# Finishing an item's maxima on VectorE and GpSimd, with at most three maxima in an attention group and one burst more in an MLP's first step

## The chip, the core and the metric

The kernel runs on one core of a Trainium2 chip. The core has a matrix engine (TensorE, here PE, with its weight loads as PEld), a vector engine (VectorE, DVE), an engine for activation functions (ScalarE, ACT), a general one (GpSimd, POOL) and one that here only issues DMAs (SyncE, SP). Each works through its own instructions in order; semaphores tie them together. Matrix products land in PSUM, eight banks of 128 × 512 float32; everything else on the chip lies in SBUF. The metric is device time in microseconds (us), the median over several runs.

## The reference

One transformer layer on 2048 rows of width 512, in float32: softmax attention with 32 heads of width 16, and then an MLP of width 1792 with SiLU, each behind a LayerNorm and added to its input.

```
x = A_x                                        # (1, 2048, 512)
h  = x + A_ref(layernorm(x), wqkv, wo)         # 32 heads of 16, no mask
h2 = h + B_ref(layernorm(h), w1, w2)           # silu(h @ w1) @ w2
A_ref: q, k, v = split(x @ wqkv); p = softmax(q @ k.T * 16**-0.5); (p @ v) @ wo
```

## The kernel before

**Stages.** First LayerNorm, transposition and the projections to q, k and v, for all rows. Queries and keys are split into a high and a low half-precision part and parked in DRAM (`qd`, `kd`). Then attention, in 32 *items*: an item is one block of 512 query rows and four heads, so eight items make a block of rows. After each block come the output projection, the second LayerNorm and the MLP for its 512 rows; those of blocks 0 to 2 lie inside attention, that of the last block at the end. The MLP of a block runs after the first 16 groups of the next block's first item, that is, at groups 144, 272 and 400 (`marks`, L670); the output projection lies in the groups just before.

**An attention group.** An item is 16 groups, one for each 128 keys, 512 groups in all, numbered g. In a group (L714 to L723) PE forms for each of the four heads the scores of 128 keys against 512 queries (`scores`, bank `ps_s`), ACT takes the exponential into `pt` (L81), and two groups later four heads' value products are added into the bank `pv` (`values`, L67). Products with `pt` are in float32, and each is recorded as two instructions, so a group has eight of them.

**The maxima.** The exponential needs the row maximum of each query's scores beforehand, so the same scores are formed once more, in the other orientation and ahead of time: `maximum` (L198) forms 128 queries against 512 keys on PE in one of three banks `ps_m` and DVE reduces it to one number (L206). An item has 64 of these. Two heads use the lower and the upper half of the matrix engine's rows; inside a group a maximum is issued right behind the scores of a head on the other half, and the two run at the same time. When an item's 64th maximum is out, `finish_max` (L210) reduces four numbers to one for each row and head (`nm`, L213), scales it and splits it into a high and a low half-precision part (`ns`, L216 and L217). Two *ticks* later (`WAIT = 2`; a tick is a group, or a step of an MLP) `place_max` (L222) transposes `ns` on PE (L70), copies it with ACT (`mt`, L227) and writes it with four DMAs on SP's queue (L231) into the rows of the item's queries `qs`, from where the score product itself subtracts the maximum. The scores of an item wait for these four DMAs. Queries and keys of five items are on the chip at a time (`RING`).

**Who forms how many maxima, and when.** 212 of the 2048 are formed in the projections. In an MLP, `weave` counts products and calls `burst(3)` at each eighth (`BESIDE_C = 8, 3`). An MLP's step f (14 of them) has twelve products of the first layer and, from f = 1, twelve of the second for f − 1. In attention a planner, `maxima(g)` (L672), says how many maxima a group gets:

```
rate = max([(64 * (n + 1) - BESIDE * sum(g <= m <= KC * n for m in marks) - at["done"])
            / max(1, KC * n - AHEAD - g) for n in range(i + 1, ITEMS)] or [0])
```

So each later item n has to be through with its maxima `AHEAD` groups before its first group, 16 n, with `BESIDE` maxima counted as done in each MLP that lies between. The largest of these demands is the rate; what it amounts to is saved up in `due`, and whole maxima are taken from it, at most four in a group. The order of the program is fixed: every instruction is issued in the order of the text on its engine.

**GpSimd's part.** It multiplies the attention output by the inverse sums (`divide`, L513) once in two items, after waiting for the DMA of `den`; in the MLPs of blocks 0 to 2 it forms the low parts of the weights, `w1l` and `w2l`, with a subtraction of two 128 × 512 tiles each (L74). In the small statistics of the LayerNorm it forms `rs` in two steps.

Of the kernel before, what the change touches and what calls it, by code (L numbers as in the profile page):

```python
# [14 lines left out]
ALU = mybir.AluOpType  # L15
# [21 lines left out]
MX = 2.0 ** 15  # L37
# [8 lines left out]
ITEMS = NB * H // 4  # L46

WAIT = 2
AHEAD = 6


BESIDE = 123
OUTPUT = 9

BESIDE_A = 7, 4
# [4 lines left out]
def attention_mlp_kernel(ctx: ExitStack, tc: tile.TileContext, x, wqkv, wo, w1, w2, out):  # L60
    nc = tc.nc
# [11 lines left out]
    def pool(op, *a, **k):  # L73
        tc.keep_in_program_order(getattr(nc.gpsimd, op)(*a, **k))  # L74


    def pin(ins):
        tc.keep_in_program_order(ins)

    def act(fn, *a, **k):  # L80
        pin(getattr(nc.scalar, fn)(*a, **k))  # L81

    def dve(fn, *a, **k):
        pin(getattr(nc.vector, fn)(*a, **k))  # L84

    def dma(*a):
        pin(nc.sync.dma_start(*a))  # L87

    def low(dst, src, high, engine="dve"):

        if engine == "pool":
            pool("tensor_tensor", dst, src, high.bitcast(F32), ALU.subtract)
        else:
            dve("tensor_tensor", dst, src, high.bitcast(F32), ALU.subtract)
# [6 lines left out]
    def product(ps, lh, ll, rh, rl, n, start=True, stop=True):  # L101

        k = 0
        for c in range(n):
            for a, b in ((lh, rh), (ll, rh), (lh, rl)):
                mm(ps, a(c), b(c), start=start and k == 0, stop=stop and k == 3 * n - 1)
                k += 1
                yield
# [11 lines left out]
    def bank(name, kind="st", dtype=F32):  # L120
        return banks[kind].tile([P, 512], dtype, tag=kind, name=name)
# [88 lines left out]
    def finish_max(i):  # L210

        nm = small.tile([P, 16], F32, name="nm")
        pin(nc.vector.tensor_reduce(nm, mx.pop(i).rearrange("p j a q k -> p (j a q) k"), axis=AX.X, op=ALU.max,  # L213
                                    negate=True))
        ns = small.tile([P, 2, 16], F16, name="ns")
        pin(nc.vector.tensor_scalar(ns[:, 0, :], nm, 1.0 / MX, None, op0=ALU.mult))  # L216
        pin(nc.vector.scalar_tensor_tensor(ns[:, 1, :], nm, 1.0 / MX, ns[:, 0, :], op0=ALU.mult, op1=ALU.subtract))  # L217
        return ns

    placed = set()  # L220
# [18 lines left out]
    at = {"item": 0, "done": 0, "half": 0, "products": 0, "step": 0, "due": 0, "mlp": False}  # L239
# [6 lines left out]
    def tick():  # L246
        at["step"] += 1
        for fn, a in agenda.pop(at["step"], ()):
            fn(*a)
# [6 lines left out]
    def one_max(half=None):  # L256

        i = next_item()
        if i == ITEMS:
            return  # L260
        if half is None:
            half = at["half"]
            at["half"] = 1 - half
        half = half if todo[i, half] else 1 - half
        at["done"] += 1
        if maximum(*todo[i, half].pop(0)):
            soon(WAIT, place_max, i, finish_max(i))
# [5 lines left out]
    def weave(steps, beside):  # L273

        for _ in steps:
            at["products"] += 1
            if beside and at["products"] % beside[0] == 0:
                burst(beside[1])


    with ExitStack() as pa:
# [142 lines left out]
        for g in range(1, NG // 2):  # L424
            for m, (b, key) in enumerate([(b, 1) for b in range(NB)] + [(b, 0) for b in range(NB)]):
# [4 lines left out]
                n = 8 * g + m - 12  # L430
# [92 lines left out]
    def load_weights(kind, f):  # L523
        if f < FC:
            w = raw_w[kind, f] = gp.tile([P, 512], F32, tag="w", name="w", bufs=4)
            if kind == "w1":
                dma(w.rearrange("p (c n) -> p c n", n=P), w1[:, f * P:(f + 1) * P].rearrange("(c p) n -> p c n", p=P))
            else:
                dma(w, w2[f * P:(f + 1) * P, :])

    def split_weights(kind, f, engine):
        if f < FC:
            w = raw_w.pop((kind, f))
            wh, wl = ws[kind, f] = [gp.tile([P, 512], F32R, name=kind + part) for part in "hl"]
            act("copy", wh, w)
            low(wl, w, wh, engine)
# [20 lines left out]
    def rows_of(b, t):  # L557
        return ot[b % 2][:, t].rearrange("p c n -> p (c n)")
# [10 lines left out]
    def mlp(b, beside):  # L569
        engine = "pool" if beside else "dve"  # L570

        first = bank("ps_w1")
        acc = [bank("ps_acc") for _ in range(3)]

        def second(f, gh, gl):
            w2h, w2l = ws.pop(("w2", f))
            if f == 0:
                acc.append(bank("ps_acc"))
            for t in range(4):
                weave(product(acc[t], lambda c: gh[:, t * P:(t + 1) * P], lambda c: gl[:, t * P:(t + 1) * P],  # L580
                              lambda c: w2h, lambda c: w2l, 1, start=f == 0, stop=f == FC - 1),
                      beside if f < FC - 1 else None)
                if f == FC - 1:
                    n = 4 * b + t
                    h = rows_of(b, t)
                    dve("tensor_tensor", h, acc[t], h, ALU.add)
                    dma(out[n * P:(n + 1) * P, :], h)

        last = None
        at["products"] = 0  # L590
        for f in range(FC):
            tick()
            load_weights("w1", f + 2)
            load_weights("w2", f + 1)
            w1h, w1l = (w.rearrange("p (c n) -> p c n", n=P) for w in ws.pop(("w1", f)))
            split_weights("w1", f + 1, engine)
            split_weights("w2", f, engine)
            ps = pv if f else first
            weave(product(ps, lambda c: w1h[:, c, :], lambda c: w1l[:, c, :],
                          lambda c: hth[:, c, :], lambda c: htl[:, c, :], DC), beside)  # L600
            g, gh, gl = (bp.tile([P, 512], dt, tag="pt", name=name)
                         for name, dt in (("g", F32), ("gh", F32R), ("gl", F32R)))
            act("activation", g, ps, AF.Silu)
            act("copy", gh, g)
            low(gl, g, gh)
            if last:
                second(*last)
            last = (f, gh, gl)
        if b < NB - 1:

            act("activation", small.tile([P, 1], F32, name="sw"), ident[:, :1], AF.Exp)
        second(*last)
# [14 lines left out]
    def finish_block(b, pending):  # L627

        act("activation", small.tile([P, 1], F32, name="sw"), ident[:, :1], AF.Silu)
        for g in pending:  # L630
            values(g)
        at["mlp"] = True
        mlp(b, BESIDE_C)
        at["mlp"] = False

    def finish_last(pending):
# [29 lines left out]
        for t in range(4):  # L666
            turn_rows(t)
        mlp(b, None)

    marks = [KC * (8 * b + 1) for b in range(1, NB)]  # L670

    def maxima(g):  # L672

        i, c = divmod(g, KC)
        if g < LAG:
            return 0
        ready = min(ITEMS, i + RING - (0 if c == KC - 1 else 1)) * 64
        rate = max([(64 * (n + 1) - BESIDE * sum(g <= m <= KC * n for m in marks) - at["done"])
                    / max(1, KC * n - AHEAD - g) for n in range(i + 1, ITEMS)] or [0])
        if ready < END:  # L680
            rate = min(rate, (ready - at["done"]) / (KC - 1 - c or KC))
        at["due"] += max(0, rate)
        n = max(0, min(4, int(at["due"]), ready - at["done"]))
        at["due"] -= n
        return n

    fixed_rows(RING - 1)
    for g in range(groups):
# [10 lines left out]
        if i in (8, 16, 24):  # L699
            b, n = i // 8 - 1, c - OUTPUT  # L700
# [8 lines left out]
        if g == groups - 4:  # L709
            for t in range(4):  # L710
                load_rows(NB - 1, t)
            for w in first_weights.values():
                load_weights(*w)
        n = maxima(g)  # L714
        for m in range(4):
            k = m ^ (g % 2)
# [41 lines left out]
```

## Time and profile before

| | |
|---|---|
| runs (three) | 1754.59, 1755.76 (median), 1760.3 us |
| the profiled execution | 1754.43 us, of which the span is 1752.7 |
| mean granted TensorE clock in it | 0.992 |
| projections of q, k, v and the start | to about 208 us |
| attention with three MLPs inside | about 208 to 1643 us |
| output and MLP of the last block | from about 1643 us |
| DVE, small operations of 32 items: L213, L216, L217 | 220, 209, 203 ns mean |
| of these, the longest single ones | 222, 886, 1061 ns |

The profile is one execution recorded instruction by instruction. A line of a time list gives the start, the time from the start of the first to the end of the last of a run of like instructions, engine, line of the kernel, operation, output and input with their shapes, and how many; in brackets stands how long the engine had been idle before and for whom. A table by stretches gives start and end, the length, then for each engine that has such instructions the busy time and their number, and last the granted clock, the DMA engines' share and GB/s. Instructions overlap on an engine: a matmul of 0.4 us is followed by the next after 0.23.

### The profile page before, as it was taken

Reading aid. Unit: us, or ns where it says so; the run is one execution under the profiler, and the core shown is the slowest. Engines: PE = TensorE matmul, PEld = TensorE weight load, DVE = VectorE, ACT = ScalarE, POOL = GpSimd, SP = SyncE. Lnnn points to the kernel's source line nnn. Section 1 sums busy time; section 2 is a strip of 40 time slices with the busy share of each in tenths; the row PEclk is TensorE's granted clock in tenths of the full one; section 3 lists DMA queues with packets and bytes.
Section 4 is the critical chain, followed back from the end, with each engine's and each line's share of the span. In section 5 each row is a group of like instructions: output and inputs, shape, how many; then the busy total and the mean of one; then the engine's idle time right before and its main releaser. Section 6 shows DMA issues by size and latency. Waiting matters only on the chain.

```text
span 1752.7 us, 28228 instructions
## 1 busy us (share of the span) xinstructions
PE 1699.7 (97%) x10466; PEld 654.2 (37%) x10466; DVE 1472.0 (84%) x2456; ACT 1263.3 (72%) x2507; POOL 208.4 (12%) x216
## 2 busy tenths in 40 slices
PE   7899999999999999999999999999999999999899
PEld 6655422222245532222245532222245532221377
DVE  6889899999978889999978899999978889994243
ACT  4223499999963369999963269999963279999643
POOL 2112210000033300000033300000033200000000
PEclk9999999999999999999999999999999999999999
DMA  6233311111113111111213111111222111100232
GB/s 183 91 87 137 113 36 44 38 39 48 51 52 100 57 45 32 35 41 44 58 48 100 55 48 30 35 45 40 61 69 82 49 45 34 36 8 11 64 90 74
DMA packets 102210, 103.10 MB, mean 59 GB/s; under 512 B 20344, under 2 KB 78776, under 8 KB 102072
## 3 DMA queue, kind: packets, MB, share of 16 engines
q1 hardware_dynamic: 102072, 101.30, 19.8%
q8 instruction: 82, 1.34, 0.3%
q14 instruction: 56, 0.46, 0.1%
HBM read 77.86 MB, written 17.30 MB: 54 GB/s over the span
## 4 chain that ended last, share of the span: by engine, by line
PE 46%; ACT 33%; DVE 18%; DMA 1%; issue 1%; SPq 1%; POOL 0%; ACTq 0%; POOLq 0%; DVEq 0%
ACT pt L81 31%; PE pv L67 20%; DVE mx L206 13%; PE ps_s L67 9%; PE ps_m L67 6%; PE ps_acc L67 5%; PE ps_wo L67 2%; DVE gl L84 2%; PE ps_v L67 2%; PE ps_qk L67 1%; ACT pvs L81 1%; DVE ot L84 1%; SPq L87 1%; PE ps_tr L70 1%; DMA w<-in_B_w_dram 0%
## 5 line engine op out<-in xcount | busy, mean ns | idle before, releaser
L206 DVE TENSOR_REDUCE mx<-ps_m 128x1 f32<-128x512 f32 x2048 | 1280.4, 683 | 114.2 <-PE ps_m L67 87.8
L81 ACT ACTIVATE pt<-ps_s 128x512 f32<-128x512 f32 x2048 | 1017.7, 646 | 31.9 <-PE ps_m L67 31.4
L67 PE MATMUL ps_s<-qs,ks 64*128 64x512 f16 x2048 | 549.9, 380 | 10.6 <-ACT pt L81 2.4
L67 PE MATMUL ps_m<-ks,qs 48*128 48x512 f16 x2048 | 531.1, 381 | 11.6 <-DVE mx L206 8.9
L67 PE MATMUL pv<-pt,va 128*17 128x512 f32 x4096 | 539.0, 599 | 0.9
L67 PEld LDWEIGHTS <-ks 64*128 64x128 f16 x2048 | 152.4, 94 | 549.9 <-issue 443.5
L67 PEld LDWEIGHTS pv<-pt,va 128*17 128x17 f32 x4096 | 68.8, 95 | 240.3 <-issue 225.9
L67 PEld LDWEIGHTS <-qs 48*128 48x128 f16 x2048 | 122.1, 94 | 82.8 <-issue 77.1
L81 ACT ACTIVATE g<-pv 128x512 f32<-128x512 f32 x52 | 31.1, 597 | 146.3 <-PE pv L67 146.3
L74 POOL TENSOR_TENSOR ot<-ot,den 128x512 f32<-128x512 f32 x15 | 19.1, 1275 | 938.3 <-DMA den<-dr 938.3
L84 DVE TENSOR_TENSOR gl<-g,gh 128x512 fp32r<-128x512 f32 x56 | 59.0, 1053 | 44.1 <-ACT gh L81 44.1
L67 PE MATMUL ps_acc<-w2h,gh 128*128 128x512 f32 x224 | 92.3, 412 | 0.0
L67 PE MATMUL ps_acc<-w2l,gh 128*128 128x512 f32 x224 | 91.6, 409 | 0.0
L81 ACT CAST w2h<-w 128x512 fp32r<-128x512 f32 x56 | 34.8, 621 | 75.2 <-POOL w1l L74 38.7
L67 PE MATMUL ps_acc<-w2h,gl 128*128 128x512 f32 x224 | 88.1, 393 | 0.0
L67 PE MATMUL pv<-hth,w1l 128*128 128x512 f32 x208 | 86.6, 416 | 0.0
L67 PE MATMUL pv<-htl,w1h 128*128 128x512 f32 x208 | 82.8, 398 | 0.0
L67 PE MATMUL pv<-hth,w1h 128*128 128x512 f32 x208 | 82.8, 398 | 0.0
L74 POOL TENSOR_TENSOR w1l<-w,w1h 128x512 fp32r<-128x512 f32 x42 | 54.7, 1301 | 165.1 <-ACT w1h L81 154.8
L81 ACT ACTIVATE ks<-ps_qk,qk_s 128x512 f32<-128x512 f32 x24 | 16.5, 689 | 70.4 <-PE ps_qk L67 70.4
L74 POOL TENSOR_TENSOR w2l<-w,w2h 128x512 fp32r<-128x512 f32 x42 | 53.6, 1277 | 59.2 <-ACT w2h L81 59.2
L67 PE MATMUL ps_qk<-xtl,wqk_h 128*128 128x512 f32 x128 | 52.8, 413 | 3.4 <-DVE xtl L84 3.4
(99 smaller groups left out, 1162.6 us busy)
## 6 DMA issues: line engine op xcount, KB each, us to landing
w<-in_B_w_dram SPq DMA_DIRECT2D x112, 256.0 KB
ks<-kd SPq DMA_DIRECT2D x120, 192.0 KB
qs<-qd SPq DMA_DIRECT2D x128, 48.0 KB
kd<-sh SPq DMA_DIRECT2D x16, 256.0 KB
qd<-sh SPq DMA_DIRECT2D x16, 256.0 KB
ot<-pvs SPq DMA_DIRECT2D x128, 32.0 KB
den<-dr SPq DMA_DIRECT2D x128, 32.0 KB
hx<-in_A_x_dram SPq DMA_DIRECT2D x16, 256.0 KB
```

The costliest lines, as they stand in the source:

```text
L67: tc.keep_in_program_order(nc.tensor.matmul(*a, **k))
L70: tc.keep_in_program_order(nc.tensor.transpose(*a))
L74: tc.keep_in_program_order(getattr(nc.gpsimd, op)(*a, **k))
L81: pin(getattr(nc.scalar, fn)(*a, **k))
L84: pin(getattr(nc.vector, fn)(*a, **k))
L87: pin(nc.sync.dma_start(*a))
L206: pin(nc.vector.tensor_reduce(mx[i][:, j, a, qt, kb:kb + 1], ps, axis=AX.X, op=ALU.max))
```

## The change

Four things are edited. In `finish_max`, DVE keeps the reduction L213; the scaling and the split into two halves go to GpSimd, as three instructions instead of two: a scaling in place, a copy into half precision and a subtraction. The planner's cap goes from four maxima in a group to three. `AHEAD` goes from 6 to 4. In the MLPs the counter of products starts at 12 in the steps f = 0 and f = 1, where it started at 0 once: in step 0 bursts come after the 4th and the 12th product instead of after the 8th, and from step 1 on they stand where they stood; that is 41 bursts in an MLP instead of 40, and `BESIDE` goes from 123 to 126. Nothing changes in the last block's MLP, which has no bursts.

```diff
-AHEAD = 6
+AHEAD = 4
-BESIDE = 123
+BESIDE = 126
@@ finish_max
         ns = small.tile([P, 2, 16], F16, name="ns")
-        pin(nc.vector.tensor_scalar(ns[:, 0, :], nm, 1.0 / MX, None, op0=ALU.mult))
-        pin(nc.vector.scalar_tensor_tensor(ns[:, 1, :], nm, 1.0 / MX, ns[:, 0, :], op0=ALU.mult, op1=ALU.subtract))
+        pool("tensor_scalar", nm, nm, 1.0 / MX, None, op0=ALU.mult)
+        pool("tensor_copy", ns[:, 0, :], nm)
+        pool("tensor_tensor", ns[:, 1, :], nm, ns[:, 0, :], ALU.subtract)
         return ns
@@ mlp
         last = None
-        at["products"] = 0
         for f in range(FC):
             tick()
+            if f < 2:
+                at["products"] = 12
@@ maxima
-        n = max(0, min(4, int(at["due"]), ready - at["done"]))
+        n = max(0, min(3, int(at["due"]), ready - at["done"]))
```

Worked through by hand, the planner's rule gives the 512 groups these numbers of maxima:

| maxima in a group | before | after |
|---|---|---|
| four | 21 groups | none |
| three | 458 | 489 |
| two | 9 | none |
| none (start and end) | 24 | 23 |

## The prediction

> **What bounds the kernel now.** I read the page first, then the instructions of PE in order of time inside attention, then DVE and GpSimd at the moments when PE's pitch breaks.
>
> ```profile
> span 1752.7 us, 28228 instructions
> PE 1699.7 (97%) x10466; PEld 654.2 (37%) x10466; DVE 1472.0 (84%) x2456; ACT 1263.3 (72%) x2507; POOL 208.4 (12%) x216
> PE 46%; ACT 33%; DVE 18%; DMA 1%; issue 1%; SPq 1%; POOL 0%; ACTq 0%; POOLq 0%; DVEq 0%
> L206 DVE TENSOR_REDUCE mx<-ps_m 128x1 f32<-128x512 f32 x2048 | 1280.4, 683 | 114.2 <-PE ps_m L67 87.8
> ```
>
> The chain changes hands between PE, ACT and DVE, so near-equal limits are at work and the pitch of a group decides. Each group of attention ends with its eight value matmuls, so the starts of these rows give the pitch. First five groups at the end, where no maxima are left; then a stretch with threes and one four:
>
> ```profile
> 1620.02 1.05 PE L67 MATMUL pv<-pt,va 128*17 128x512 f32 x8
> ...
> 1629.82 1.05 PE L67 MATMUL pv<-pt,va 128*17 128x512 f32 x8
> ```
>
> ```profile
> 714.74 1.05 PE L67 MATMUL pv<-pt,va 128*17 128x512 f32 x8
> ...
> 716.70 1.05 PE L67 MATMUL pv<-pt,va 128*17 128x512 f32 x8
> ...
> 718.89 0.37 PE L67 MATMUL ps_m<-ks,qs 48*128 48x512 f16 x1 [0.16 <-DVE mx L206]
> 719.20 1.05 PE L67 MATMUL pv<-pt,va 128*17 128x512 f32 x8
> ...
> 721.21 1.05 PE L67 MATMUL pv<-pt,va 128*17 128x512 f32 x8
> ```
>
> Without maxima a group takes 9.80/5 = 1.96 us, with three also 1.96 (716.70 − 714.74): three maxima are free, since they run beside the scores. The group with four takes 2.50 and the next 2.01: together **0.58 over**. PE stands at the fourth `ps_m` until DVE returns one of three banks. DVE needs 1280.4/2048 = 0.63 for each, 0.60 where they follow without a break (five in 3.07, in the last row of the finished item below: (3.07 − 0.68)/4), so 1.8 of 1.96 with three and 2.4 with four. An item's boundary costs something of its own, which stays:
>
> ```profile
> 702.59 1.05 PE L67 MATMUL pv<-pt,va 128*17 128x512 f32 x8
> ...
> 708.86 1.05 PE L67 MATMUL pv<-pt,va 128*17 128x512 f32 x8
> ```
>
> 6.27 − 3 × 1.96 = 0.39, where the next item's first values wait for ACT to copy `pv`. Now the four steady stretches of attention, clear of output and restart (scores only; four to a group):
>
> ```profile
> 236.50:490.85 254.35, 133.40 (x500) 247.21 (x501) 1.00 0.16 42
> 642.50:883.37 240.87, 125.81 (x472) 232.96 (x471) 1.00 0.16 43
> 1032.77:1274.03 241.26, 124.95 (x472) 233.50 (x472) 1.00 0.16 44
> 1428.36:1640.60 212.24, 110.76 (x424) 209.06 (x424) 1.00 0.12 32
> ```
>
> They hold 125, 118, 118 and 106 groups and 8, 7, 7 and 6 boundaries. 948.72 − 467 × 1.96 − 28 × 0.39 leaves **22.5 us of excess**. Counting through the planner's rule gives 20 fours there (21 in all) and 20 finished items. The fours are 20 × 0.58 = 11.6; up to 0.5 is the pitch's third decimal; the rest, 10.4, is 0.52 for each finished item. One of them:
>
> ```profile
> 717.39 5.95 DVE L206 TENSOR_REDUCE mx<-ps_m 128x1 f32<-128x512 f32 x9
> 723.37 0.22 DVE L213 TENSOR_REDUCE nm<-mx 128x16 f32<-128x64 f32 x1
> 723.63 0.17 DVE L216 TENSOR_SCALAR ns<-nm 128x16 f16<-128x16 f32 x1
> 723.84 0.17 DVE L217 SCALAR_TENSOR_TENSOR ns<-nm,ns 128x16 f16<-128x16 f32 x1
> 723.93 3.07 DVE L206 TENSOR_REDUCE mx<-ps_m 128x1 f32<-128x512 f32 x5
> ```
>
> Nine maxima end at 723.34; the next would have started some 0.08 before that end (as 723.93 lies 0.08 before the end of L217) and starts 0.67 late.
>
> **Part 1, no fours.** By the planner's rule the threes go from 458 groups to 489, fours from 21 to 0, twos from 9 to 0. Threes and twos cost the same to 0.1 us. Gain in the four stretches 11.6; PE's own matmuls for the moved maxima ran beside scores and cost nothing.
>
> **Part 2, two of the three small operations leave DVE.** After the change the next maximum follows L213: 723.37 + 0.22 − 0.08 = 723.51 against 723.26, **0.25 late instead of 0.67**. If the item ends with a group's third maximum, DVE's spare 0.16 of that group absorbs most, 0.10 left; else 0.25. Of 19 such items after the change 6 are thirds: 13 × 0.25 + 6 × 0.10 = 3.9 where 10.4 was. So the 22.5 becomes 3.9 + 0.5, a gain of **18.1** with part 1. At the three restarts after an MLP one finished item each saves 0.4, but two groups there get a third maximum at 0.60 while DVE is behind: nothing net.
>
> What GpSimd adds is latency. The transposition that PE runs two ticks later waits for `ns`. An item that ended third, and the one above, which ended first:
>
> ```profile
> 458.80 0.22 DVE L213 TENSOR_REDUCE nm<-mx 128x16 f32<-128x64 f32 x1
> ...
> 459.79 0.10 PEld L70 LDWEIGHTS <-ns 128*32 128x32 f16 x1 [0.31 <-DVE ns L217]
> 460.22 0.22 PE L70 MATMUL ps_n<-ident_h,ns 128*32 128x128 f16 x1
> 726.65 0.22 PE L70 MATMUL ps_n<-ident_h,ns 128*32 128x128 f16 x1
> ```
>
> From L213's end the transposition starts 1.20 later for a third (its weights need 0.1 of that, so 1.1 may pass), 3.06 for a first; a second, one maximum of 0.60 later, has about 2.4. The saved 0.4 comes off both ends of firsts and seconds: 2.6 and 2.0. Behind the waiting load stand all of PE's next scores and, for them, ACT. No row shows these operations on GpSimd; nearest are those on one element per partition:
>
> ```profile
> 1663.37 0.42 POOL L74 TENSOR_SCALAR rs<-mv 128x1 f32<-128x1 f32 x1 [0.90 <-DVE mv L84]
> 1663.87 0.57 POOL L74 TENSOR_TENSOR rs<-rs,expo 128x1 f32<-128x1 f32 x1
> ```
>
> I take 0.42 for the scaling, 0.30 for the copy (one input, no arithmetic) and 0.40 for the subtraction (below the power's 0.57), and 0.07 for each of four hand-overs (1663.87 − 1663.37 − 0.42 = 0.08): a chain of 1.40. Of the 23 items finished inside attention eight are thirds, eight seconds and seven firsts; the eight thirds are late by 0.3 each: **+2.4**. Bounds: 0.22 a step, the shortest scaling in the trace's rows of `rs`, gives about 0.95 and nothing; 0.57 a step gives 2.0, 8 × 0.9 = 7. GpSimd's queue is free for it: its multiplications by `den` are issued five groups or more ahead of a finished item or after it, and the weight splits stand in MLPs, where two ticks are two steps.
>
> [...]
>
> In the third MLP the two operations collide with GpSimd:
>
> ```profile
> 1365.60 0.89 DVE L216 TENSOR_SCALAR ns<-nm 128x16 f16<-128x16 f32 x1
> 1365.19 1.27 POOL L74 TENSOR_TENSOR w2l<-w,w2h 128x512 fp32r<-128x512 f32 x1 [1.62 <-ACT w2h L81]
> 1367.36 0.37 PE L67 MATMUL ps_m<-ks,qs 48*128 48x512 f16 x1 [1.46 <-DVE mx L206]
> 1360.00:1380.00 20.00, 18.54 (x73) 10.11 (x72) 14.73 (x24) 5.44 (x10) 5.08 (x4) 0.91 0.03 12
> ```
>
> L216 ends as GpSimd's 1.27 end, PE stands 1.46, and then the granted clock falls: 0.91 over 20 us is 1.8 us at full speed lost. With both operations gone the stand shrinks by about 1.0 and the fall, most of it, goes too: **−2.5** (0 to −2.8).
>
> **Part 3, one burst more in the first step of three MLPs.** A burst here:
>
> ```profile
> 523.43 0.39 PE L67 MATMUL ps_w<-hth,w1l 128*128 128x512 f32 x1
> 523.75 0.60 PE L67 MATMUL ps_m<-ks,qs 48*128 48x512 f16 x3
> 524.28 0.50 PE L67 MATMUL ps_w<-htl,w1h 128*128 128x512 f32 x1
> 524.62 0.40 PE L67 MATMUL ps_w<-hth,w1h 128*128 128x512 f32 x1
> ```
>
> 1.19 from 523.43 to 524.62, two steps that take 0.47 without it: 0.72. Bursts will stand after products 4 and 12 of the first step and 4 of the next, so two are only four products apart, 4 × 0.23 + 0.72 = 1.65, under the 1.8 that DVE needs, with `gl` (0.69) between. I add 0.6: 1.3 × 3 = **+3.9** (0.7 to 2.0 each).
>
> **Part 4, AHEAD 4 and the cap.** Items become ready later. By the rule item 24's maxima end in group 382 and it is placed at the tick of 384, whose scores need it; before it was placed at 379. Items 16 and 8 keep 2 and 3 groups, the others 4 or more or an MLP. What a placement needs:
>
> ```profile
> 726.81 0.39 PE L67 MATMUL ps_s<-qs,ks 64*128 64x512 f16 x1
> 727.22 2.75 SPq L231 DMA_DIRECT2D qs<-mt  x4
> 1652.82 0.87 SPq L87 DMA_DIRECT2D den<-dr  x2
> 1655.38 0.69 DVE L84 TENSOR_TENSOR ot<-ot,den 128x512 f32<-128x512 f32 x1 [4.31 <-DMA den<-dr]
> ```
>
> The fourth issue starts about 0.63 before 729.97; the last `den` of 32 KB is used some 2.1 after its issue starts, one of 2 KB I put at 1.5. So the scores could go at 730.85 instead of 726.81: **+4.0** for item 24 (3.5 to 4.7), everything behind them waiting in order. Item 16 has 3.92 of cover: **+0.1**. A stand of 1.46 was followed by a fall of the clock above, worth 1.7: **+1.7** (0 to 3.4).
>
> [...]
>
> **Sum:** −18.1 + 2.4 − 2.5 + 3.9 + 4.0 + 0.1 + 1.7 = −8.5, on the profiled execution's 1754.43 (1752.7 span, 1.7 around it): **1745.9**. The median of the runs, 1755.76, lies 1.3 above that execution.
>
> **Rivals.** (a) *The chain on GpSimd is long.* At three steps of 0.57 the lateness is 7: 1750.5. The point from which it decides is a chain of 2.2: 8 × 1.1 + 8 × 0.2 = 10.4 of the 10.9 that are left without it; from 2.6 the kernel is slower by over 0.3%: at 0.9 a step, 3.0 in all, 8 × 1.9 + 8 × 1.0 + 7 × 0.4 = 26 makes 1769.5. For it: the power's 0.57 on one element; against: nothing in the trace near 0.9 for so little data. (b) *The finishing cost isn't the two operations* but L213's wait for the last maximum and the transposition; then 10.4 stays and the time is 1752.4. Against: 723.93 follows L217 at once. (c) *Late placements cost more*: if SP's queue is behind at 254 as well, item 16 stands 3 and drops the clock, and 24's fall lasts twice: 1745.9 + 3 + 1.7 + 1.7 = 1752.3. Against: the loads in that item are issued by group 253, and no `dn` or `ot` then.
>
> **Chances.** About 0.3% (5.3 us) is what a measurement of this kernel tells from no change. Forecast 0.60, within 1740 to 1750; (a) at 2.0 to 2.5 0.15 and beyond 0.08; (b) 0.08; (c) 0.09. Faster is nearly all of the forecast (0.58), half of the nearer part of (a) (0.07) and the lower edges of (b) and (c) (0.06): 0.71; slower the far part of (a) and 0.01 of the rest, 0.09; same the 0.20 between. The cheap ends (no lateness, 0.7 a burst, no fall) give 1739; range 1738 to 1754.
>
> **What would show it.** Right: no group over 2.3 us off the boundaries, groups after a finished item under 2.25, one stand of 4 us before group 384 on `qs<-mt`, L213 followed directly by maxima. Wrong: the loads of `ns` waiting over 1 us for GpSimd; stands at other items; MLPs longer by over 2 us each.

## The result and the profile after

| | before | after |
|---|---|---|
| median of the runs | 1755.55 us (1754.59 to 1760.3, four runs) | 1744.85 us (1743.0 to 1747.01, four runs) |
| ratio, 95% interval | | 0.9936 (0.9925 to 0.9948) |
| profiled execution, its span | 1754.43, 1752.7 us | 1747.01, 1745.2 us |

The kernel is 0.64% faster; 1745.9 was forecast. The four runs come in two pairs, 1743.0 and 1743.0, 1746.7 and 1747.0; the mean granted clock is 0.990 and 0.989 in the first and 0.987 in the second, and the profile is of the second.

The page of the changed kernel:

```profile
span 1745.2 us, 28284 instructions
PE 1696.8 (97%) x10466; PEld 655.6 (38%) x10466; DVE 1453.6 (83%) x2392; ACT 1258.9 (72%) x2507; POOL 229.5 (13%) x312
ACT 45%; PE 44%; DVE 8%; DMA 1%; issue 1%; SPq 1%; POOL 0%; ACTq 0%; POOLq 0%; DVEq 0%
L67 PE MATMUL ps_s<-qs,ks 64*128 64x512 f16 x2048 | 552.7, 381 | 14.9 <-DMA qs<-mt 4.7
L67 PE MATMUL ps_m<-ks,qs 48*128 48x512 f16 x2048 | 526.0, 383 | 2.2 <-DVE mx L206 0.8
L74 POOL TENSOR_SCALAR nm<-nm 128x16 f32<-128x16 f32 x32 | 9.4, 294 | 728.8 <-DVE nm L213 712.1
```

DVE's part of the chain went from 18% to 8%, and a new wait stands with the scores, for the DMAs `qs<-mt`. The four steady stretches of attention, scores only, as before:

```profile
236.44:486.18 249.74, 133.00 (x500) 246.35 (x501) 1.00 0.16 43
638.63:875.15 236.52, 125.42 (x472) 232.12 (x470) 1.00 0.15 44
1027.78:1270.07 242.29, 126.88 (x472) 232.49 (x471) 0.99 0.16 43
1421.18:1632.58 211.40, 110.88 (x424) 209.17 (x426) 1.00 0.12 32
```

939.95 − 467 × 1.96 − 28 × 0.39 leaves 13.7 us of excess against 22.5. In the third stretch 6.7 of it stand around group 384, so without that stand the excess is 7.0. An item that ends first in its group now looks like this, on DVE, on GpSimd and on PE:

```profile
329.49 0.22 DVE L213 TENSOR_REDUCE nm<-mx 128x16 f32<-128x64 f32 x1
329.63 1.88 DVE L206 TENSOR_REDUCE mx<-ps_m 128x1 f32<-128x512 f32 x3
329.80 0.25 POOL L74 TENSOR_SCALAR nm<-nm 128x16 f32<-128x16 f32 x1 [27.79 <-DVE nm L213]
330.11 0.20 POOL L74 CAST ns<-nm 128x16 f16<-128x16 f32 x1
330.39 0.22 POOL L74 TENSOR_TENSOR ns<-nm,ns 128x16 f16<-128x16 f32 x1
332.35 0.22 PE L70 MATMUL ps_n<-ident_h,ns 128*32 128x128 f16 x1
```

The next maximum starts 0.14 after L213, inside its own duration. From the end of L213 (329.71) the chain on GpSimd takes 0.90 us; the transposition comes 2.64 after it, as the prediction's 2.6 had it. In attention the 0.90 to 0.91 is the same for every item. The group behind such an item takes 2.31 us, a little over the 2.25 that the prediction named as a sign.

The stand at group 384, PE and SP, and the clock around it (the last column but two is the granted clock):

```profile
1243.57 0.22 PE L70 MATMUL ps_n<-ident_h,ns 128*32 128x128 f16 x1
1244.13 2.75 SPq L232 DMA_DIRECT2D qs<-mt  x4
1248.07 0.58 PE L67 MATMUL ps_s<-qs,ks 64*128 64x512 f16 x1 [4.28 <-DMA qs<-mt]
1249.89 1.91 PE L67 MATMUL pv<-pt,va 128*17 128x512 f32 x8
1240.00:1260.00 20.00, 15.72 (x104) 3.35 (x99) 12.56 (x22) 13.80 (x30) 0.67 (x3) 0.83 0.14 40
1246.18:1253.01 6.83, 4.94 (x22) 1.17 (x22) 2.49 (x4) 2.71 (x6) 0.00 (x0) 0.50 0.26 78
```

The value products of group 384 take 1.91 instead of 1.05. A clock of 0.83 over 20 us is 6.8 us at half speed; the last row is these 6.83 us. They begin 2.4 us into the stand, so that only 4.9 of them fall on PE's work.

Where the profiled executions differ, stretch by stretch, from the starts of the groups' first scores:

| stretch | foreseen | measured |
|---|---|---|
| four steady stretches without the stand | −18.1 + 2.4 | −15.5 |
| third MLP, with its extra burst | −2.5 + 1.3 | −2.5 |
| the extra bursts, first and second MLP | +1.3 each | +0.1 each |
| the stand and the clock behind it | +4.1 + 1.7 | +4.7 + 2.0 |
| the first four, four and five groups after the three MLPs | 0 | +0.8, +2.9, −0.7 |
| all else (projections, first groups, output, last block) | 0 | about +0.8 |
| sum | −8.5 | −7.5 |

### The profile page after: what moved, and what is told of

The parts are those of the page before. It is cut to its first block, busy times and chain, and to the rows that moved or that the text cites. A ratio compares the mean times of both kernels' runs of the same rounds, so it can differ in the third digit from the quotient of the medians.

```text
span 1745.2 us, 28284 instructions
## 1 busy us (share of the span) xinstructions
PE 1696.8 (97%) x10466; PEld 655.6 (38%) x10466; DVE 1453.6 (83%) x2392; ACT 1258.9 (72%) x2507; POOL 229.5 (13%) x312
## 3 DMA queue, kind: packets, MB, share of 16 engines
q8 instruction: 82, 1.34, 0.3%
## 4 chain that ended last, share of the span: by engine, by line
ACT 45%; PE 44%; DVE 8%; DMA 1%; issue 1%; SPq 1%; POOL 0%; ACTq 0%; POOLq 0%; DVEq 0%
ACT pt L81 44%; PE pv L67 15%; PE ps_acc L67 7%; PE ps_m L67 6%; PE ps_qk L67 6%; DVE mx L206 5%; PE ps_s L67 5%; PE ps_wo L67 2%; PE ps_v L67 2%; DVE gl L84 1%; PE ps_w L67 1%; ACT pvs L81 1%; PE ps_tr L70 1%; DVE st L84 0%; DVE ot L84 0%
## 5 line engine op out<-in xcount | busy, mean ns | idle before, releaser
L74 POOL TENSOR_SCALAR nm<-nm 128x16 f32<-128x16 f32 x32 | 9.4, 294 | 728.8 <-DVE nm L213 712.1
L84 DVE TENSOR_TENSOR gl<-g,gh 128x512 fp32r<-128x512 f32 x56 | 53.3, 952 | 41.6 <-ACT gh L81 41.6
```

## The experiments

Ratios are to the kernel before, run on the same chip. The *excess* is that of the four steady stretches, worked out as above from the starts of the scores in each profile.

| kernel | median us | ratio (95%) | excess us |
|---|---|---|---|
| changed, two operations back on VectorE | 1753.09 | 0.9988 (0.9978 to 0.9998) | 20.8, of it 7.1 the stand |
| before, two operations on GpSimd | 1745.99 | 0.9947 (0.9930 to 0.9964) | 17.0 |
| before, one burst more in step 0 | 1754.81 | 0.9993 (0.9982 to 1.0004) | 17.9 |
| before, item 24 placed late | 1762.71 | 1.0046 (1.0028 to 1.0064) | 28.4 |
| changed, maxima from group 0 | 1734.38 | 0.9871 (0.9856 to 0.9886) | 7.5 |
| changed, long chain on GpSimd | 1747.44 | 0.9954 (0.9939 to 0.9969) | 19.5, of it 7.1 the stand |
| changed, from group 0, one maximum at restarts | 1739.77 | 0.9912 (0.9897 to 0.9927) | 7.4 |
| before, one burst more in step 5 | 1756.11 | 1.0002 (0.9990 to 1.0013) | 18.0 |
| changed, from group 0, operations on VectorE | 1747.13 | 0.9952 (0.9932 to 0.9971) | 12.4 |

**The two operations back on VectorE.**

```diff
-        pool("tensor_scalar", nm, nm, 1.0 / MX, None, op0=ALU.mult)
-        pool("tensor_copy", ns[:, 0, :], nm)
-        pool("tensor_tensor", ns[:, 1, :], nm, ns[:, 0, :], ALU.subtract)
+        pin(nc.vector.tensor_scalar(ns[:, 0, :], nm, 1.0 / MX, None, op0=ALU.mult))
+        pin(nc.vector.scalar_tensor_tensor(ns[:, 1, :], nm, 1.0 / MX, ns[:, 0, :], op0=ALU.mult, op1=ALU.subtract))
```

> The changed kernel with the scaling and the split of an item's maxima back on VectorE, all else as changed. Theory (the two operations delay VectorE by 0.4 us more for each of some 20 items): the four steady stretches hold 5 to 7 us more excess than the changed kernel's (6.7 us without the stand before group 384), about 0.69 us after an item that ends first or second in a group and 0.50 after a third; total 1750 to 1753 us. Rival (the cost of finishing is the reduction L213 and the transposition, not the two operations): excess the same within 1 us, total 1743 to 1747.

The excess without the stand is 13.7 against 7.0, 6.7 more; after an item that ended first or second the pitch is over by 0.69, with GpSimd by 0.35; after a third by 0.49 and 0.24. The total, 1753.09, is in the theory's range. The rival that the cost lies in L213 and the transposition falls. The MLPs change as well, which the theory didn't have: the first two are 1.0 and 0.6 longer than the changed kernel's, and the third takes 118.55 against 115.43, since the collision is back.

**Only the two operations on GpSimd.** The same edit the other way, in the kernel before.

> The kernel before with only the scaling and the split moved to GpSimd; the fours, AHEAD and the bursts as before. Theory: finishing an item costs 0.35 instead of 0.6 to 0.7 us, and the collision in the third MLP is gone: 1754.4 less 6 to 7 less 2.5, so 1745 to 1748 us; excess of the steady stretches 15 to 16 of 22.5 us; third MLP 115.5 us instead of 117.9. Rival (GpSimd's latency makes the transposition wait): 1752 us or more, with the load of ns idle for GpSimd.

1745.99 us, and the third MLP takes 114.9 instead of 117.9 from its preceding scores to the next. The excess is 17.0, one above the range: the fours are still there. In this profile the second MLP is 2.5 longer than before; in its third step the products from 923.81 to 926.37 start 0.43 apart instead of 0.23, a slow stretch that neither theory had. In attention `ns` is ready 0.91 after L213 and the transposition is nowhere late for it.

**One burst more, in the kernel before.**

```diff
         for f in range(FC):
             tick()
+            if f < 2:
+                at["products"] = 12
```

> The kernel before with only the counter of products started at 12 in the first two steps of the MLPs, so one burst more in each; BESIDE stays 123. By the planner's rule 15 fours instead of 21. Theory of the prediction (a burst costs 0.72 us and crowds the next): each MLP 1.3 us longer, 116.9 us against 115.6, and the gain from the fours (3.5 us) is given back: 1754 to 1756 us. Rival (its 1.2 us come back in the next steps, where VectorE's gl and GpSimd's weight splits no longer run at the same time): MLPs within 0.3 us of before, 1750 to 1753 us.

The first two MLPs are 0.2 and 0.8 longer at their end. The third is 0.2 longer too, but that hides more: at its 169th product it is 1.6 behind the kernel before (57.75 us after its first product against 56.11), and the collision that follows costs 1.4 less here, with a stand of 1.16 instead of 1.46. So a burst costs 0.2, 0.8 and 1.6; neither the theory's 1.3 for each nor the rival's 0.3 fits all three. The total, 0.9 below before with an interval that takes in 1, tells nothing by itself. Inside the second MLP the burst does cost 1.2 at first: the seventeenth product of the two layers starts 6.39 after the first, before 5.20. By the forty-ninth the first MLP has 0.15 of it left, 16.73 against 16.58. What gives it back shows on DVE, first in the kernel before, then in the changed one, at the same point of the first MLP:

```profile
527.47 3.79 DVE L206 TENSOR_REDUCE mx<-ps_m 128x1 f32<-128x512 f32 x6
532.19 1.34 DVE L84 TENSOR_TENSOR gl<-g,gh 128x512 fp32r<-128x512 f32 x1 [0.93 <-ACT gh L81]
533.45 3.67 DVE L206 TENSOR_REDUCE mx<-ps_m 128x1 f32<-128x512 f32 x6
```

```profile
525.80 1.89 DVE L206 TENSOR_REDUCE mx<-ps_m 128x1 f32<-128x512 f32 x3 [0.45 <-PE ps_m L67]
527.61 0.68 DVE L84 TENSOR_TENSOR gl<-g,gh 128x512 fp32r<-128x512 f32 x1
528.38 1.89 DVE L206 TENSOR_REDUCE mx<-ps_m 128x1 f32<-128x512 f32 x3
```

Before, DVE stood 0.93 for ACT's `gh` and then took 1.34 for `gl` instead of 0.68, beside GpSimd's subtractions for `w2l` and `w1l` (531.69 to 534.67), while the next burst's maxima waited behind it and PE for them. In the changed kernel, with the burst earlier, `gh` is there when DVE comes to it, and `gl` takes 0.68. In this experiment's first MLP `gh` is there too and `gl` takes 1.02; in its second DVE still stands 0.61 and `gl` takes 1.36, and there the 0.8 stays. In its third an item is finished in step 0, beside GpSimd:

```profile
1303.07 1.29 POOL L74 TENSOR_TENSOR w2l<-w,w2h 128x512 fp32r<-128x512 f32 x1
1303.23 1.15 DVE L217 SCALAR_TENSOR_TENSOR ns<-nm,ns 128x16 f16<-128x16 f32 x1
```

L217 takes 1.15 where 0.17 is usual, and ends with GpSimd's subtraction. In step 0 of the changed kernel's first MLP an item is finished as well; there the operations wait for GpSimd and the next maximum follows L213 at once. So the burst comes back in all three MLPs only together with the move to GpSimd: it leaves 0.1, 0.1 and 0.5 in the changed kernel (the 0.5 at the third's 169th product), against 0.2, 0.8 and 1.6 here and 1.1 and 0.7 in the first two MLPs with the operations back on VectorE. What sets the smaller of these costs isn't shown.

**The extra burst in step 5 instead.**

```diff
             split_weights("w2", f, engine)
+            if f == 5 and beside:
+                burst(3)
             ps = pv if f else first
```

> The kernel before with one burst of three maxima more at the head of step 5 of each of the three MLPs, four products from the bursts on both sides; the first step as before. It tells where an extra burst costs. Theory (the one in the first step came back because VectorE stood waiting there for ACT's copy gh; in step 5 it has little such waiting): each MLP about 0.7 to 1.3 us longer than 115.6 us, still so at its end. Rival (an extra burst is taken back anywhere): MLPs within 0.3 us of 115.6.

The second MLP, from its first product to the next scores, in the kernel before, the changed one, and this one:

```profile
914.15 0.50 PE L67 MATMUL ps_w<-hth,w1h 128*128 128x512 f32 x1
...
1024.79 0.39 PE L67 MATMUL ps_s<-qs,ks 64*128 64x512 f16 x1
```

```profile
906.18 0.49 PE L67 MATMUL ps_w<-hth,w1h 128*128 128x512 f32 x1
...
1016.91 0.39 PE L67 MATMUL ps_s<-qs,ks 64*128 64x512 f16 x1
```

```profile
915.08 0.49 PE L67 MATMUL ps_w<-hth,w1h 128*128 128x512 f32 x1
...
1027.82 0.39 PE L67 MATMUL ps_s<-qs,ks 64*128 64x512 f16 x1
```

110.64, 110.73 and 112.74: in step 5 a burst costs 2.1 and keeps it, more than the 0.7 to 1.3 expected; in step 0 of the changed kernel it costs 0.1. The first MLP is 3.2 longer (the mean granted clock of this execution is 0.990, of the kernel before's 0.992); the third is 0.4 longer at its end, but 1.9 behind at its 169th product, before a collision that costs 1.5 less here. So an extra burst isn't taken back anywhere. In the same kernel step 0 left 0.2, 0.8 and 1.6: clearly less in the first two MLPs, hardly in the third.

**Item 24 placed late, in the kernel before.**

```diff
-            soon(WAIT, place_max, i, finish_max(i))
+            soon(7 if i == 24 else WAIT, place_max, i, finish_max(i))
```

> The kernel before with item 24 placed seven ticks after its maxima end instead of two, so at the tick of group 384, whose scores need it; nothing else changed. Theory: PE stands 4.0 to 4.3 us before group 384 and then has its clock halved for 3.4 to 6.8 us (1.7 to 3.4 us): 5.7 to 7.7 us more, 1761 to 1763 us. [...]

```profile
1258.23 0.37 PE L67 MATMUL ps_s<-qs,ks 64*128 64x512 f16 x1 [4.50 <-DMA qs<-mt]
```

The third stretch takes 247.15 instead of 241.26, 5.9 more, and the median is 7.0 above the before of the same chip, both within the theory's 5.7 to 7.7. The two groups behind the stand are slow (pitches 3.28 and 2.22 instead of 1.96; in the changed kernel 3.66 and 2.56), and the value products of group 384 take 1.91 instead of 1.05, as long as in the changed kernel, where the granted clock was 0.50 over them.

**Maxima from group 0.**

```diff
-AHEAD = 4
+AHEAD = 6
@@ maxima
-        if g < LAG:
-            return 0
```

> The changed kernel with maxima formed from group 0 on (the planner's rule of none in the first two groups taken out) and AHEAD 6 again, so that by the rule item 24 is placed two groups before its scores, not at their tick, and item 16 three. Theory (the stand before group 384 and the clock behind it cost 7.0 us in the changed kernel): the stand goes to 0.4 us or less, the excess of the third stretch from 8.3 to 1.3 to 2 us, and the total is 6 to 7 us lower, 1737 to 1740 us, if three more maxima in the first two groups cost nothing there. Rival (the stand only moves to another transfer or item): 1743 us or more.

```profile
1238.74 0.37 PE L67 MATMUL ps_s<-qs,ks 64*128 64x512 f16 x1 [0.41 <-DMA qs<-mt]
```

That is group 384 here: 0.41 instead of 4.28, the value products behind it take 1.05, and the third stretch is 5.9 shorter than the changed kernel's. The total is 1734.38, 10.5 below the changed kernel and lower than the range. Some 6 of it are the stand and its clock; in the profiles 4.6 more are the first two restarts, 9.24 and 8.03 us against 10.96 and 10.88; in the changed kernel's profile the granted clock is 0.50 for 6.83 us at each of the two (631.79 to 638.62 and 1020.90 to 1027.73), and the mean over the execution is 0.987 there and 0.993 here. This version beats both. The run changes the first groups and `AHEAD` together; what either does alone isn't shown.

**A long chain on GpSimd.**

```diff
         pool("tensor_copy", ns[:, 0, :], nm)
+        for _ in range(4):
+            pool("tensor_copy", ns[:, 0, :], nm)
```

> The changed kernel with the copy into half precision done five times on GpSimd instead of once, which leaves the output as it is: the chain from the end of L213 grows from 0.91 to about 2.0 us. Theory (only what passes the transposition's own time counts: 1.1, 2.0 and 2.6 us for an item that ends third, second, first in a group): the eight thirds are late by 0.9 to 1.0 us each, seconds and firsts not: 7 to 8 us more, 1751 to 1753 us. Rival (the latency of GpSimd counts for every item): 1.1 us for each of 23 items, 25 us more, 1770 us; or it counts for none, 1745 us.

The chain is 2.0. After thirds the transposition waits:

```profile
287.81 0.23 PE L70 MATMUL ps_n<-ident_h,ns 128*32 128x128 f16 x1 [0.70 <-POOL ns L74]
```

There the two groups mostly cost 0.68 more than with the short chain (2.88 and 1.96, where 2.00 and 2.16 stood; at the least 0.37, at the most 0.78); after firsts and seconds the pitch is 2.31 in both. The excess is 5.8 more, somewhat under the 7 to 8 foreseen. The total misses the range: 1747.44 instead of 1751 to 1753, only 2.6 above the changed kernel's median of its two pairs of runs; in the profiles the first two restarts take 4.4 less here (8.03 and 9.44). By the excess and the rows the threshold is as theory had it: a latency within the transposition's own lag costs nothing, one beyond it does, and both rivals fall. By the total alone the second rival, 1745, would not be refuted.

**Fewer maxima at the restarts.**

```diff
-        n = max(0, min(3, int(at["due"]), ready - at["done"]))
+        n = max(0, min(1 if g in marks else 3, int(at["due"]), ready - at["done"]))
@@ mlp, weave
+            at["every"] = 6 if f == 1 and b < NB - 1 else 0
-            if beside and at["products"] % beside[0] == 0:
+            if beside and at["products"] % (at["every"] or beside[0]) == 0:
```

> The kernel with maxima from group 0 and AHEAD 6, and with one maximum instead of three in the first group after each of the three MLPs; to make up for them the second step of an MLP has a burst at each sixth product instead of each eighth (one burst more), with BESIDE 129. Theory (VectorE is behind at the restart by four additions of 0.69 us, and the clock falls there in some executions): the four groups from the restart take 7.2 to 7.9 us instead of 8 to 11, with fewer falls of the clock; 1 to 5 us less than with maxima from group 0 alone, 1733 to 1738 us. Rival (the extra burst costs its 0.7 us and PE waits at the restart anyway): no difference or slower by 1 to 2 us.

It is 5.4 slower than with maxima from group 0 alone. The second and third MLP are 1.0 and 1.4 longer, the first 6.0 (the mean granted clock of this execution is 0.990, with maxima from group 0 alone 0.993); the second restart takes 7.98 against 8.03, both near the 7.90 that it takes in the first experiment at a granted clock of 1.00. So the two maxima fewer bring nothing in this restart, the one that can be compared, and the burst costs; both parts of the theory fail, and the rival was still too mild.

**Only the fours gone.** The kernel with maxima from group 0, with the first experiment's edit.

> The kernel with maxima from group 0 and AHEAD 6, but with the scaling and the split of an item's maxima on VectorE as before: so the fours are gone, the bursts are in, no item is placed at the tick that needs it, and only the move to GpSimd is undone. Theory (fours 11 us, the two operations 6 to 8 us with the collision in the MLP, nothing between them): excess of the four stretches 11 to 13 us against 22.5 before and 7.5 with the move; total 1740 to 1744 us. Rival (fours and finishing share one delay, so that either alone brings most of it): excess 8 us or less, 1737 us or less.

The excess, 12.4, is in the theory's range: against 22.5 the fours are worth 10.1, and the move to GpSimd another 4.9. Alone the move was worth 5.5 (the second experiment), so the two nearly add up; the rival falls. The total, 1747.13, is 3 above the range; in these two profiles the projections take 2.1 more, the second MLP 1.0 and the first two restarts 2.5 (mean granted clock 0.991 against 0.993). Whether the projections gain from the move isn't settled: attention starts at 204.9 to 207.6 us in the profiles with the operations on GpSimd and at 206.5 to 209.8 with them on VectorE.

## Why the prediction was right

**The fours and the finished items: right.** The two terms, together −18.1 with 2.4 given back, came out as −15.5. The mechanism, DVE's 0.60 for each maximum against a pitch of 1.96, holds: with threes alone no group breaks the pitch except at boundaries and finished items. In size the shares differ. The 20 fours are worth 10.1 by the last experiment, 0.5 each and not 0.58. A finished item costs 0.35, not 0.25 (0.24, not 0.10, for a third): 13 × 0.35 + 6 × 0.24 = 6.0 where 3.9 stood.

**The chain on GpSimd: the mechanism right, the size too large.** Put at 1.40, it is 0.91: the scaling 0.25, the copy 0.20 and the subtraction 0.22 are all shorter than the nearest rows of before (0.42, which is an addition, and 0.57, on one element per partition). It ends inside the 1.1 that a third allows, so the 2.4 is 0. That and the dearer finish cancel. The subtraction, its one operation on two tensors, takes 0.22 against 0.17 for L217 on VectorE, and the whole chain costs nothing. The threshold of 1.1 and 2.0, on which rival (a) hung, is shown by the long chain.

**The collision in the third MLP: right, and a little larger.** It is 117.93 to 115.43 between the scores on both sides, with the extra burst inside; with only the operations moved, and no burst, 114.88. So the collision was worth about 3, and the burst took some 0.5 of it back. PE stands for over 1 us in the third MLP in no profile with the operations on GpSimd, and in five of the six with both on VectorE. Behind the stand of 1.46 in the kernel before the granted clock was 0.50 for 3.42 us (1368.58 to 1372.00), 1.7 us at full speed. In the first, third and fourth experiments the stands are 1.16 to 1.25. In the third and fourth the collision costs 1.4 and 1.5 less than before (1.6 − 0.2 and 1.9 − 0.4), of which the shorter stand is 0.2 to 0.3; by estimate from these figures, most of the 1.7 didn't occur there, so it is no fixed part of the collision. A slow stretch in another MLP shows in the second experiment, where the longest wait just before it is 0.52.

**The burst: the step that failed.** "I add 0.6: 1.3 × 3 = +3.9": the 0.72 and the crowding are there, 1.2 us after sixteen products, but the step took for granted that what PE loses in step 0 stays lost. DVE stood idle for ACT's `gh` early in the MLP and was late afterwards; the burst used this time, and 0.1 remained in the first two MLPs and 0.5 in the third. In step 5 the same burst costs 2.1 for good. The prediction also priced the burst apart from the move to GpSimd; with the finishing operations on VectorE it costs 0.2 to 1.6.

**The stand: right, the clock too.** 4.28 against 4.0, and the fall of the clock took 2.0 against 1.7. In the changed kernel the granted clock of 0.50 began 2.4 us into the stand and lasted 6.83. In the four profiles with a stand of this length, the changed kernel, the operations back on VectorE, item 24 placed late and the long chain, the stand and the groups behind it cost 6.7, 7.1, 5.9 and 7.1, each time more than the 4.28 and 4.50 that the stand itself took in the first and the third of these.

**The restarts: put at nothing, +2.9 in this profile.** The extra maxima and the dearer or cheaper finish do nearly cancel: the first experiment has the same plan of maxima, and its first two restarts take 8.44 and 7.90, where the changed kernel's took 10.96 and 10.88. The second restart in both, the changed kernel first and with its stretch of half clock, the granted clock as third last number:

```profile
1016.90:1026.40 9.50, 9.46 (x41) 2.27 (x44) 7.78 (x14) 7.62 (x16) 0.00 (x0) 0.71 0.26 96
1020.90:1027.73 6.83, 6.83 (x27) 0.94 (x25) 4.29 (x8) 4.49 (x9) 0.54 (x3) 0.50 0.00 0
```

```profile
1021.50:1031.00 9.50, 9.46 (x60) 2.62 (x60) 9.17 (x19) 9.06 (x19) 0.00 (x0) 1.00 0.26 96
```

PE is busy all the time in both, and does 41 matmuls in one and 60 in the other. What decides between them isn't settled; PE has no single gap over 0.5 us there in either.

So the sum was right to 1 us by luck, because two errors of opposite sign cancelled in the profiled execution: the bursts and the collision, +1.4 foreseen and −2.3 measured, were 3.7 too dear, and the restarts with all else 3.7 too cheap. One sum at the edge doesn't come out either: the cheap ends (−2.4, −1.8 for bursts of 0.7, −1.7) make 1740.0 and not 1739. Of the rivals, (b) is refuted by the first experiment, (c) didn't occur (item 16's scores wait 0.38 and the granted clock is 1.00 from 850 to 880), and (a) has its price nearly right, 5.8 for the 7 foreseen at a chain of 2.0, but not its premise.

## What to carry to other kernels

Where several engines run at nearly one pitch, price an edit by what it does to the one group in which an engine overruns its buffers, not by its mean load: a fourth maximum of 0.60 us cost some 0.5, and three cost nothing. Work moved to an engine on which it takes longer (0.90 us from the end of L213 to `ns` on GpSimd, 0.42 on VectorE) was free here as long as its latency ended inside a lag that was already in the program; write that lag down for each position before moving. Parts of an edit that use the same spare time of an engine shouldn't be priced apart: the extra burst was nearly free in every MLP only with the finishing off VectorE. And an ahead-of-time schedule that is squeezed to smooth it should be checked for its tightest deadline: one item placed at the tick that needs it cost 6.7 us of the gain, and five maxima formed in the first two groups, where none had been, together with the old `AHEAD` brought that back.

## What the runs showed of the hardware that was not expected

A scaling, a copy and a subtraction on 128 × 16 elements take 0.25, 0.20 and 0.22 us on GpSimd, while an addition on 128 × 1 elsewhere in the kernel before takes 0.42 in the median (0.22 at the least). The granted clock fell to half at a restart in which PE was busy throughout by the record (0.50 over 6.83 us at the changed kernel's second, with PE busy 6.83), and not in another profile with the same plan of maxima (1.00 over 9.50 us in the first experiment). An operation on 128 × 16 elements that takes 0.17 us on VectorE took 1.15 in the third experiment, beside a GpSimd subtraction on 128 × 512 that took 1.29.
